# An FFT filter woven into a mixture layer: side products put behind other hosts, and their loads moved

## The chip, the cores and the metric

One core of one Trainium2 chip. TensorE (PE) multiplies, VectorE (DVE), ScalarE (ACT) and GpSimd (POOL) work on elements, SyncE (SP) issues nearly all transfers. The metric is the device time of one execution in microseconds, as a median of runs.

## What is computed

Eight batches of 3072 x 256 go through three stages:

```python
X = np.fft.rfft(x, axis=1)                        # stage 1: filter
y = np.fft.irfft(X * (filt_r + 1j * filt_i), n=x.shape[1], axis=1)
h = np.maximum(x @ w_in, 0.0)                     # stage 2: x is y, d_ff = 2048
x = h * h @ w_out
logits = x @ phi                                  # stage 3: 8 experts, 4 slots each
d = softmax(logits, over tokens); slot_input = d.T @ x
slot_out = per expert: np.maximum(slot_input @ w1, 0) @ w2
return softmax(logits, over slots) @ slot_out
```

## The kernel before

**Tiling.** 24576 tokens are 48 chunks of 512, six to a batch. A chunk takes eight pairs, a pair makes two blocks p0 and p1 of 128 hidden features: 12 full-array matmuls of 512 columns (L594 to L596, three products of split values). p0 and p1 each have one PSUM bank, so a block can start only when ACT's relu (L601) has read the one before. Square of p0 is on ACT (L603), square of p1 on POOL (L605), both transposed by DVE (L622). Eight squared blocks feed sixteen logit products (L663), whose result L leads to the softmax over tokens: evac_l (L712, L713), gather (L723, L724), emax (L729, L731), expo (L747), rescale (L753), turn_e, turn_l, slot_in (L794, the slots product), accum; then row_max, row_exp, row_out and store_c for the softmax over slots. The transposed hidden rows reach slot_in by 16 transfers a chunk (move, L651), each with an SP issue.

**The filter.** Its batch of 3072 points is factored into n1 = 128 by n2 = 24. mm_a (L165) is the forward product over n1, behind fold_x (L155 on DVE, L156 on POOL) and load_x, followed by evac_a (L172) and store_a (L181) to DRAM tensor S. load_s2 (L206) reads S turned; mm_b (L299) is the forward product over n2, then filt (L310), join (L319), mm_g2 (L218), evac_g2 (L228), store_g2 to DRAM tensor G. load_g (L460) reads G as gin for one group of 512 tokens, that is one chunk; mm_y (L514) is the inverse over n1, then even_y (L522), two unfolds (L531), and lead_y (L539, ACT) and rest_y (L546, POOL), which write the high and low half of xo, the next chunk's input, for k = 0 and 1. Groups 0, 1 and 6 take two transposing products (mm_ai, L478) instead.

**Order.** All engines run in the order in which the program issues instructions, written by hand. Time is counted in positions t: a pair is two, a half block 0.5, a chunk 16, a batch 96. Five streams of steps (dsp, mv, late, fft, w) each hold (t, step); at every half block run_streams fires what is due, steps without PSUM banks before the half block too, those with banks after it. Five side banks are shared. Positions below are counted within a chunk, so 9.5 is behind the second half of the fifth pair's p1. The logits come at 1.5 and 9.5; the slots product of the chunk before follows at 9.5, the gather at 3.5. Moves are due at 10 to 11.5, 14, 14.5, 2 and 2.5. In the steady state of batches 3 to 7, y comes at 9.5 behind the slots product; the b products (four a batch) once at 1.5 behind the logits and three times at 6 alone; the a products (three a batch) at 6 twice and at 1.5 once; g2 at 1.5. fft_events has the steps of one batch with three lists (TA: load, fold, product of each third; TB: b products; TG: g2) and lead times before them (LEAD: weights w, v, filter f, S). What a batch's filter does is laid over the chunks of the batch before.

Of the kernel before, what the change touches and what calls it, by code (L numbers as in the profile page):

```python
# [22 lines left out]
NCH = NB * NCB  # L23
# [15 lines left out]
def body(tc, x, cA, cAf, fwp, fwd, ivp, inv, flt, cst, w_in, w_out, phi, w1, w2, out):  # L39
# [83 lines left out]
    def fft_events(b, pl, put, TA, TB, TG, n, st):  # L123
# [263 lines left out]
        if b == 0:  # L387
# [21 lines left out]
            for i in range(8):  # L409
                put((.38, .4, .42, .44)[i] if i < 4 else F(i - 4) + 2.6, load_f, i)  # L410
                T = (16.8, 17.2, 20, 22.4, 24.9, 25.3, 27.4, 27.8)[i]
                for s in range(2):
                    put(T + .1 * s, mm_t, i, s)
                    put(T + .3 + .1 * s, evac_t, i, s)
                put(F(i) - 1.2, mm_b, i)
# [4 lines left out]
                put((29.85, 32.3, 34.75, 37.2, 39.9, 41.5, 44.6, 40.5)[i], mm_g, i)  # L420
                T = (31.1, 33.6, 36.1, 38.6, 41.2, 44.7, 45.9, 42.4)[i]
                for c in range(4):
                    put(T, evac_g, i, c)
                put(T + 1.25, store_g, i)
            return

        for s, (TL, TF, T) in enumerate(TA):
            put(TL, load_x, s)
            for k in range(2):
                put(TF + k, fold_x, s, k)  # L430
                for g in range(2):
                    put(T + 0.5 + (0 if T % 16 == 6 else 0.5) * k, evac_a, s, k, g)
                put(T + 2 + 0.5 * k, store_a, s, k)
            put(T, mm_a, s)
        LW, LV, LF, LS = n["lead"]
        for j in range(4):
            T = TB[j]
# [10 lines left out]
            T = TG[j]  # L448
# [5 lines left out]
    def out_events(b, st, late):  # L454

        def load_g(g):
            if b + g:
                t = G["mlp"].tile([128, 4, D], F32, tag="gin", name="gin", bufs=2)
                src, o = (st["G1"], 0) if (b, g) == (0, 1) else (st["G"], 4 * g - 8 * (b == 0))
                sync.dma_start(out=t, in_=src[:, o:o + 4, :])  # L460
            else:
                t = scratch("gi", 1, [128, 4, D])
                sync.dma_start(out=t[0:96], in_=st["Gu"])
                sync.dma_start(out=t[96:128], in_=st["Gz"])
            st["gi", g] = t

        def warm():

            p = side()
            for _ in range(6):  # L470
                pe.matmul(p[:, 0:416], cI, cst_t[:, 0:416], start=True, stop=True)
            done(p)

        def mm_ai(g, k):
            t = st["gi", g]
            p = side()
            for a in range(4):
                pe.matmul(  # L478
                    p[:, 128 * a:128 * a + 128], t[:, a, 128 * k:128 * k + 128], cI,
                    start=True, stop=True,  # L480
                )
            st["ai", g, k] = p

        def lead_ai(g, k):
            if k == 0:
                xo[b * NCB + g] = G["mlp"].tile([128, 2, 2, CH], F32R, tag="xo", name="xo", bufs=2)
            act.activation(
                out=xo[b * NCB + g][:, 0, k, :].rearrange("p (q a t) -> p a q t", q=4, a=4),
                in_=st["ai", g, k].rearrange("p (a q t) -> p a q t", a=4, q=4), func=ACTF.Copy,
            )  # L490

        def rest_ai(g, k):
            o = xo[b * NCB + g]
            p = st.pop(("ai", g, k))
            hi, lo = (
                a[:, n, k, :].rearrange("p (q a t) -> p a q t", q=4, a=4)
                for n, a in enumerate((o.bitcast(F32), o))
            )
            vec.tensor_tensor(
                out=lo, in0=p.rearrange("p (a q t) -> p a q t", a=4, q=4), in1=hi, op=ALU.subtract  # L500
            )
            done(p)

        def mm_y(g):
            t = st["gi", g]
            st["y", g] = p = [side() for e in range(2)]
            for a in range(4):
                for k in range(2):
                    for e in range(2):
                        for d in range(2):  # L510
                            rows = slice(64 * e, 64 * e + 64)
                            o = 128 * k + 64 * d
                            y = p[e][64 * d:64 * d + 64, D * k:D * k + D]
                            pe.matmul(  # L514
                                y.rearrange("p (q a t) -> p a q t", q=2, a=4)[:, a], t[rows, a, o:o + 64],
                                cI[rows, 0:64],
                                start=True, stop=True, skip_group_check=True, tile_position=(64 * e, 64 * d),
                            )

        def even_y(g):  # L520
            p = st["y", g][0]
            act.activation(  # L522
                out=st["gi", g][:, 2:4, :], in_=p.rearrange("p (k c) -> p k c", k=2), func=ACTF.Copy
            )
            done(p)

        def unfold(g, op):
            t = st["gi", g]
            p = st["y", g][1]
            o = t[:, 0:2, :] if op == ALU.add else t[:, 2:4, :]  # L530
            vec.tensor_tensor(out=o, in0=t[:, 2:4, :], in1=p.rearrange("p (k c) -> p k c", k=2), op=op)  # L531
            if op != ALU.add:
                done(p)

        def lead_y(g, k):
            if k == 0:
                xo[b * NCB + g] = G["mlp"].tile([128, 2, 2, CH], F32R, tag="xo", name="xo", bufs=2)
            o = xo[b * NCB + g][:, 0, k, :].rearrange("p (h c) -> p h c", h=2)
            act.activation(out=o, in_=st["gi", g][:, k::2, :], func=ACTF.Copy)  # L539

        def rest_y(g, k):
            o = xo[b * NCB + g]
            hi, lo = (
                a[:, n, k, :].rearrange("p (h c) -> p h c", h=2) for n, a in enumerate((o.bitcast(F32), o))
            )
            gps.tensor_tensor(out=lo, in0=st["gi", g][:, k::2, :], in1=hi, op=ALU.subtract)  # L546

        for g in range(NCB):
            if 6 * b + g not in (0, 1, 6):
                T = 96 * b + 16 * g - 6.5  # L550
                late(max(T - 19.5, 13.5), load_g, g)
                late(T, mm_y, g)
                late(T + 0.5, even_y, g)
                late(T + 1, unfold, g, ALU.add)
                late(T + 1, unfold, g, ALU.subtract)
                for k in range(2):
                    late(T + 2 + 2 * k, lead_y, g, k)
                    late(T + 2.5 + 2 * k, rest_y, g, k)
                continue
            T = 96 * b + 16 * g - 4  # L560
            put = late
            if T < 0:
                def put(t, fn, *a):
                    put0(ST["G0"] + ST["Gd"] * (t + 7), fn, *a)
            put(T - (5 if (b, g) == (0, 1) else 3), load_g, g)
            if T < 0:
                put(T - 1, warm)
            for k in range(2):
                put(T + k, mm_ai, g, k)
                put(T + k + 0.5, lead_ai, g, k)  # L570
                put(T + k + 0.5, rest_ai, g, k)
# [126 lines left out]
    def dispatch_events(c, put):  # L698
        q = 16 * (c + 1) + (2 if c else 6)
# [203 lines left out]
        else:  # L903
            put(q + 7.5, slot_in)
            put(q + 9, accum)
        put(q + 11, row_max)
        put(q + 13, row_exp)
        put(q + 14, row_out)
        put(q + 17, store_c)


    def f64(t, a, e):
# [192 lines left out]
    with tc.manual_schedule():  # L1105
        put, late = stream("fft"), stream("late")
# [24 lines left out]
        for n in range(4):  # L1131
# [2 lines left out]
                wput(WO[n][1][k], conv_wo, n, k)  # L1134

        LEAD = [
            [[6.5, 6.5, 9.5, 9.5], [10, 7.5, 8, 10], [5, 6, 6.5, 6.5], [5.5, 10.5, 10, 10]],
            [[5.5, 7.5, 15.25, 15.25], [6.5, 12.5, 13.5, 13.5], [5, 5.5, 10, 10], [5.5, 13, 15.25, 15.25]],
            [[20.25] + [15.25] * 3, [13.5] * 4, [20.5, 10, 10, 10], [6, 15.25, 15.25, 15.25]],
        ]  # L1140

        opened = False
# [6 lines left out]
        for b in range(1, NB):  # L1149
            st = {}  # L1150
            if b == 1:
                when = ([(22, 24.5, 26.5), (24, 29, 33.5), (27.5, 32, 36.5)], [47, 54.5, 65.5, 76.5], [53, 61.5, 70.5, 81.5])
            elif b == 2:
                when = ([(-19, -15.5, -10), (-11, -7, -3), (-5.5, -3, 0)], [13.5, 22, 38, 54], [18.5, 33.5, 49.5, 65.5])
            else:
                when = ([(-41, -31, -26), (-23, -19, -14.5), (-22.5, -15.5, -10)], [1.5, 22, 38, 54], [17.5, 33.5, 49.5, 65.5])
            fft_events(b, lambda: G["fft"], stream("fft", 96 * (b - 1)), *when, dict(f=3, u=8, c=2, lead=LEAD[min(b, 3) - 1]), st)
            out_events(b, st, late)
        for c in range(NCH - 1):
# [241 lines left out]
        for g in range(NG):  # L1401
            b, o = divmod(g, N2 // 4)
# [171 lines left out]
```

## Time and profile before

| | |
|---|---|
| median of 3 runs | 1855.48 us (1854.55 to 1858.27) |
| profiled execution | 1859.09 us, its span 1857.3 us |
| granted TensorE clock, mean | 0.996 |
| busy: PE, DVE, ACT, POOL | 98%, 65%, 56%, 42% of the span |
| chain that ended last | PE 84%, DMA 5%, DVE 3% |
| SP's DMA queue | 78.7% of 16 engines' span |

The span is what the profiler recorded of the profiled execution; its own time is 1.8 us longer. PE's busy share counts matmuls from start to modelled end, and these overlap; a pause between two starts shows as idle time in the timeline, with the releaser behind the arrow. A timeline row has start, duration, engine, line, operation, output and inputs, count.

### The profile page before, as it was taken

What the parts mean: (1) busy time and instruction counts of PE and PEld (TensorE: products, weight loads), DVE (VectorE), ACT (ScalarE), POOL (GpSimd) and SP (SyncE); (2) the same over time, 40 slices, a digit from 0 to 9 for tenths busy, and PEclk for the clock granted to TensorE, in tenths of its full rate; (3) what the DMA queues carried; (4) which work ended last, traced back from release to release, by engine and by line L of the source; (5) the groups of instructions that cost most, each with busy time, mean ns of one, the idle gap of its engine ahead of it and who ended that gap; (6) DMA issues with size and microseconds to landing.
All of it is one profiled execution on the core that took longest, in us unless ns stands there. A gap on an engine that the chain in (4) does not pass through costs nothing.

```text
span 1857.3 us, 42036 instructions
## 1 busy us (share of the span) xinstructions
PE 1812.1 (98%) x16326; PEld 1192.9 (64%) x16326; DVE 1212.9 (65%) x2267; ACT 1033.4 (56%) x1930; POOL 776.3 (42%) x812
## 2 busy tenths in 40 slices
PE   9899999999999999999999999999999999999987
PEld 6666666666666666666666666666566666666555
DVE  7856666676666666666667666666666756565558
ACT  6755555556555564555655555556555555555445
POOL 4043543454444534544444444354344443333224
PEclk9999999999999999999999999999999999999999
DMA  8669989878777896888778787687878666675999
GB/s 309 205 184 281 257 234 269 247 212 238 230 213 203 227 273 165 224 243 214 234 220 222 209 253 220 189 229 217 247 199 240 200 169 182 171 206 153 247 338 383
DMA packets 245813, 425.02 MB, mean 229 GB/s; under 512 B 25712, under 2 KB 103664, under 8 KB 245616
## 3 DMA queue, kind: packets, MB, share of 16 engines
q1 hardware_dynamic: 244744, 421.13, 78.7%
q8 instruction: 130, 2.13, 0.5%
q10 hardware_dynamic: 728, 1.15, 0.2%
q14 instruction: 67, 0.55, 0.1%
q0 software_dynamic: 144, 0.07, 0.0%
HBM read 151.71 MB, written 77.59 MB: 123 GB/s over the span
## 4 chain that ended last, share of the span: by engine, by line
PE 84%; DMA 5%; DVE 3%; SPq 2%; issue 2%; ACT 1%; POOL 1%; POOLq 0%; DVEq 0%; ACTq 0%
PE p L594 18%; PE p L595 17%; PE p L596 17%; PE L L663 9%; PE sd L794 8%; PE sd L218 3%; PE sd L299 3%; PE sd L514 2%; PE sd L165 2%; DMA f<-S 2%; SPq L651 1%; DMA hd<-hT 1%; DVE ct L1208 1%; PE pt L1197 1%; PE pt L1410 1%
## 5 line engine op out<-in xcount | busy, mean ns | idle before, releaser
L605 POOL TENSOR_TENSOR h<-h 128x512 f32<-128x512 f32 x375 | 395.1, 1054 | 837.0 <-ACT h L601 747.5
L601 ACT ACTIVATE h<-p 128x512 f32<-128x512 f32 x768 | 459.0, 598 | 348.9 <-PE p L596 334.5
L622 DVE STREAM_TRANSPOSE hT<-h 128x512 f32<-128x512 f32 x736 | 485.3, 692 | 250.4 <-ACT h L603 230.4
L594 PE MATMUL p<-xo,wiH 128*128 128x512 f32 x1534 | 621.7, 405 | 0.1
L595 PE MATMUL p<-xo,wiH 128*128 128x512 f32 x1534 | 605.6, 395 | 7.2 <-POOL xo L546 7.2
L596 PE MATMUL p<-xo,wiL 128*128 128x512 f32 x1534 | 605.8, 395 | 0.0
L594 PEld LDWEIGHTS p<-xo,wiH 128*128 128x128 f32 x1534 | 288.1, 188 | 122.4 <-issue 43.9
L595 PEld LDWEIGHTS p<-xo,wiH 128*128 128x128 f32 x1534 | 288.6, 188 | 70.0 <-POOL xo L546 9.4
L596 PEld LDWEIGHTS p<-xo,wiL 128*128 128x128 f32 x1534 | 288.3, 188 | 68.4
L603 ACT ACTIVATE h<-h 128x512 f32<-128x512 f32 x393 | 248.4, 632 | 12.5
L319 POOL TENSOR_TENSOR u<-u 128x256 f32<-128x256 f32 x224 | 160.5, 739 | 114.9 <-DVE u L310 114.9
L663 PE MATMUL L<-h,wf 128*32 128x512 f32 x1536 | 186.9, 599 | 2.2 <-DVE wf L1021 1.8
L531 DVE TENSOR_TENSOR gin<-gin,sd 128x512 f32<-128x512 f32 x90 | 61.8, 687 | 182.7 <-ACT gin L522 181.2
L522 ACT ACTIVATE gin<-sd 128x512 f32<-128x512 f32 x45 | 26.9, 598 | 256.7 <-PE sd L514 256.7
L794 PE MATMUL sd<-hd,eT 128*32 128x512 f32 x1472 | 166.3, 592 | 0.0
L310 DVE TENSOR_TENSOR u<-sd,f 128x512 f32<-128x512 f32 x240 | 152.7, 675 | 11.5 <-PE sd L299 10.1
L546 POOL TENSOR_TENSOR xo<-gin,xo 128x512 fp32r<-128x512 f32 x90 | 119.3, 1325 | 0.0
L794 PEld LDWEIGHTS sd<-hd,eT 128*32 128x32 f32 x1472 | 47.8, 110 | 110.1 <-issue 106.8
L228 ACT ACTIVATE f<-sd 128x512 f32<-128x512 f32 x112 | 61.1, 610 | 79.8 <-PE sd L218 79.8
L713 DVE TENSOR_TENSOR lo<-L,lp 128x512 fp32r<-128x512 f32 x47 | 32.3, 688 | 107.4 <-ACT lp L712 107.4
L663 PEld LDWEIGHTS L<-h,wf 128*32 128x32 f32 x1536 | 40.0, 109 | 96.2 <-issue 91.4
L770 DVE STREAM_TRANSPOSE eT<-et 32x128 f32<-32x128 f32 x184 | 72.0, 391 | 1.9
(161 smaller groups left out, 1596.2 us busy)
## 6 DMA issues: line engine op xcount, KB each, us to landing
hd<-hT SPq DMA_DIRECT2D x736, 256.0 KB
f<-flt SPq DMA_DIRECT2D x28, 1024.0 KB
gin<-G SPq DMA_DIRECT2D x47, 512.0 KB
out<-w1t SPq DMA_DIRECT2D x47, 512.0 KB
f<-x SPq DMA_DIRECT2D x84, 256.0 KB
S<-f SPq DMA_DIRECT2D x42, 512.0 KB
f<-S SPq DMA_DIRECT2D x112, 192.0 KB
G<-f SPq DMA_DIRECT2D x112, 192.0 KB
```

Source lines behind the costliest of these rows:

```text
L310: vec.tensor_tensor(out=u, in0=p.rearrange("p (h d) -> p h d", d=D), in1=f[:, 2 * r + k:2 * r + k + 1, :].to_broadcast([128, 2, D]), op=AL ...
L319: gps.tensor_tensor(out=a[:, h, :], in0=a[:, h, :], in1=b[:, 1 - h, :], op=ALU.add if h else ALU.subtract)
L546: gps.tensor_tensor(out=lo, in0=st["gi", g][:, k::2, :], in1=hi, op=ALU.subtract)
L594: pe.matmul(p, wh, x[:, 0, kk, :], start=(kk == 0), stop=False)
L595: pe.matmul(p, wh, x[:, 1, kk, :], start=False, stop=False)
L596: pe.matmul(p, wl, x[:, 0, kk, :], start=False, stop=(kk == 1))
L601: act.activation(out=h, in_=p, func=ACTF.Relu, scale=2.0 ** -8)
L603: act.activation(out=h, in_=h, func=ACTF.Square)
L605: gps.tensor_tensor(out=h, in0=h, in1=h, op=ALU.mult)
L622: vec.transpose(hT[c, f // 8][:, f // 4 % 2, :, o:o + 128], h2[P, k].rearrange("p (b t) -> p b t", b=4))
L663: pe.matmul(lg[c][32 * n:32 * n + 32, :], wf[:, f, :], h2.pop((P + n // 2, n % 2)), start=(f < 4), stop=(f >= FT - 4), tile_position=(0, 3 ...
L794: pe.matmul(S[32 * n:32 * n + 32, :], e[:, 32 * t:32 * t + 32], v, start=(t == 0), stop=(t == 3), tile_position=(0, 32 * n),)
```

## The change

The b products of every batch from the second on come at 9.5, behind the slots product; two of the three a products too, the other at 1.5 behind the logits. y comes at 3.5 directly behind the gather, but for groups 2, 3 and 6. Group 6 (first of the second batch) goes by mm_y like the others. The loads of S, weights, filter, x and G come due between 3 and 6, the folds at 6, 7 and 12, 13. An a product at 9.5 has its copies to SBUF (evac_a) two by two at 11.5 and 13.5 and its stores at 13 and 15. row_max, row_exp and row_out come 2.5 later, store_c 1 later, but for the last two chunks.

```diff
--- before.py
+++ after.py
@@ -428,9 +428,10 @@
             put(TL, load_x, s)
             for k in range(2):
                 put(TF + k, fold_x, s, k)
+                slow = T % 16 == 9.5
                 for g in range(2):
-                    put(T + 0.5 + (0 if T % 16 == 6 else 0.5) * k, evac_a, s, k, g)
-                put(T + 2 + 0.5 * k, store_a, s, k)
+                    put(T + (2 + 2 * k if slow else 0.5 + 0.5 * k), evac_a, s, k, g)
+                put(T + (3.5 + 2 * k if slow else 2 + 0.5 * k), store_a, s, k)
             put(T, mm_a, s)
         LW, LV, LF, LS = n["lead"]
         for j in range(4):
@@ -546,9 +547,9 @@
             gps.tensor_tensor(out=lo, in0=st["gi", g][:, k::2, :], in1=hi, op=ALU.subtract)
 
         for g in range(NCB):
-            if 6 * b + g not in (0, 1, 6):
-                T = 96 * b + 16 * g - 6.5
-                late(max(T - 19.5, 13.5), load_g, g)
+            if 6 * b + g > 1:
+                T = 96 * b + 16 * g - {2: 9, 3: 6.5, 6: 6.5}.get(6 * b + g, 12.5)
+                late(max(96 * b + 16 * g - {6: 10, 7: 24}.get(6 * b + g, 26), 13.5), load_g, g)
                 late(T, mm_y, g)
                 late(T + 0.5, even_y, g)
                 late(T + 1, unfold, g, ALU.add)
@@ -562,7 +563,7 @@
             if T < 0:
                 def put(t, fn, *a):
                     put0(ST["G0"] + ST["Gd"] * (t + 7), fn, *a)
-            put(T - (5 if (b, g) == (0, 1) else 3), load_g, g)
+            put(T - (5 if g else 3), load_g, g)
             if T < 0:
                 put(T - 1, warm)
             for k in range(2):
@@ -903,10 +904,11 @@
         else:
             put(q + 7.5, slot_in)
             put(q + 9, accum)
-        put(q + 11, row_max)
-        put(q + 13, row_exp)
-        put(q + 14, row_out)
-        put(q + 17, store_c)
+        d = 2.5 if c < NCH - 2 else 0
+        put(q + 11 + d, row_max)
+        put(q + 13 + d, row_exp)
+        put(q + 14 + d, row_out)
+        put(q + 17 + (d > 0), store_c)
 
 
     def f64(t, a, e):
@@ -1134,9 +1136,9 @@
                 wput(WO[n][1][k], conv_wo, n, k)
 
         LEAD = [
-            [[6.5, 6.5, 9.5, 9.5], [10, 7.5, 8, 10], [5, 6, 6.5, 6.5], [5.5, 10.5, 10, 10]],
-            [[5.5, 7.5, 15.25, 15.25], [6.5, 12.5, 13.5, 13.5], [5, 5.5, 10, 10], [5.5, 13, 15.25, 15.25]],
-            [[20.25] + [15.25] * 3, [13.5] * 4, [20.5, 10, 10, 10], [6, 15.25, 15.25, 15.25]],
+            [[6.5, 6.5, 9.5, 9.5], [10, 7.5, 8, 7.5], [5, 6, 6.5, 6.5], [5.5, 10.5, 10, 10]],
+            [[6] * 4, [13.5] * 4, [14, 5.5, 5.5, 5.5], [4, 6.5, 6.5, 6.5]],
+            [[6] * 4, [13.5] * 4, [21, 5.5, 5.5, 5.5], [6.5] * 4],
         ]
 
         opened = False
@@ -1149,11 +1151,11 @@
         for b in range(1, NB):
             st = {}
             if b == 1:
-                when = ([(22, 24.5, 26.5), (24, 29, 33.5), (27.5, 32, 36.5)], [47, 54.5, 65.5, 76.5], [53, 61.5, 70.5, 81.5])
+                when = ([(22, 24.5, 26.5), (24, 29, 33.5), (27.5, 32, 36.5)], [47, 54.5, 65.5, 76.5], [53, 61.5, 73.5, 81.5])
             elif b == 2:
-                when = ([(-19, -15.5, -10), (-11, -7, -3), (-5.5, -3, 0)], [13.5, 22, 38, 54], [18.5, 33.5, 49.5, 65.5])
+                when = ([(-19, -15.5, -12.5), (-13, -10, -6.5), (-8, -4, 1.5)], [9.5, 25.5, 41.5, 57.5], [17.5, 33.5, 49.5, 65.5])
             else:
-                when = ([(-41, -31, -26), (-23, -19, -14.5), (-22.5, -15.5, -10)], [1.5, 22, 38, 54], [17.5, 33.5, 49.5, 65.5])
+                when = ([(-29, -26, -22.5), (-28, -20, -14.5), (-13, -10, -6.5)], [9.5, 25.5, 41.5, 57.5], [17.5, 33.5, 49.5, 65.5])
             fft_events(b, lambda: G["fft"], stream("fft", 96 * (b - 1)), *when, dict(f=3, u=8, c=2, lead=LEAD[min(b, 3) - 1]), st)
             out_events(b, st, late)
         for c in range(NCH - 1):
```

## Rows read from the trace of the kernel before

**Rows 1.** which lines PE waited for, whole span; us in total, times, longest us.

```profile
PE p L595 <- POOL xo L546: 7.2, 5, 1.4
...
PE sd L299 <- DMA f<-S: 4.1, 9, 1.0
...
PE sd L478 <- DMA gin<-G: 0.8, 1, 0.8
```

**Rows 2.** timeline of PE, start and duration in us, at one xo stall.

```profile
1318.91 0.40 PE L594 MATMUL p<-xo,wiH 128*128 128x512 f32 x1
1320.75 0.50 PE L595 MATMUL p<-xo,wiH 128*128 128x512 f32 x1 [1.44 <-POOL xo L546]
```

**Rows 3.** timeline of PE around a later L299 bundle of that batch.

```profile
1439.15 0.40 PE L596 MATMUL p<-xo,wiL 128*128 128x512 f32 x1
...
1439.48 1.96 PE L299 MATMUL sd<-f,fw 48*32 48x256 f32 x64
1441.36 0.50 PE L594 MATMUL p<-xo,wiH 128*128 128x512 f32 x1
...
1441.70 0.39 PE L595 MATMUL p<-xo,wiH 128*128 128x512 f32 x1
```

**Rows 4.** timeline of POOL at the same xo stall.

```profile
1313.75 1.04 POOL L605 TENSOR_TENSOR h<-h 128x512 f32<-128x512 f32 x1 [8.60 <-ACT h L601]
1314.75 1.35 POOL L546 TENSOR_TENSOR xo<-gin,xo 128x512 fp32r<-128x512 f32 x1
1316.73 1.30 POOL L156 TENSOR_TENSOR f<-f 128x512 f32<-128x512 f32 x1 [0.63 <-DMA hd<-hT]
1317.99 1.49 POOL L605 TENSOR_TENSOR h<-h 128x512 f32<-128x512 f32 x1
1319.44 1.26 POOL L546 TENSOR_TENSOR xo<-gin,xo 128x512 fp32r<-128x512 f32 x1
```

**Rows 5.** timeline of PE at the first L299 bundle of the last batch.

```profile
1360.08 0.59 PE L299 MATMUL sd<-f,fw 48*32 48x256 f32 x2
...
1363.73 0.50 PE L594 MATMUL p<-xo,wiH 128*128 128x512 f32 x1
```

**Rows 6.** timeline of SP's queue, time of issuing, ahead of that bundle.

```profile
1336.76 0.32 SPq L181 DMA_DIRECT2D S<-f  x1
1345.85 8.15 SPq L651 DMA_DIRECT2D hd<-hT  x8
1354.05 3.38 SPq L206 DMA_DIRECT2D f<-S  x4
```

**Rows 7.** timeline of ACT, one chunk.

```profile
1295.78 0.60 ACT L601 ACTIVATE h<-p 128x512 f32<-128x512 f32 x1
1296.28 0.68 ACT L747 ACTIVATE et<-sd,nm 128x512 f32<-128x512 f32 x1
1296.84 0.20 ACT L747 ACTIVATION_READ_ACCUMULATOR et<-sd,nm 128x1 f32 x1
...
1300.69 0.28 ACT L753 ACTIVATE sc<-nm 128x1 f32<-128x1 f32 x1
...
1311.41 0.60 ACT L601 ACTIVATE h<-p 128x512 f32<-128x512 f32 x1 [0.93 <-PE p L596]
1312.04 0.63 ACT L603 ACTIVATE h<-h 128x512 f32<-128x512 f32 x1
1312.58 0.61 ACT L539 ACTIVATE xo<-gin 128x512 fp32r<-128x512 f32 x1
```

**Rows 8.** timeline of PE in that chunk.

```profile
1303.34 1.92 PE L663 MATMUL L<-h,wf 128*32 128x512 f32 x16
...
1309.71 0.50 PE L594 MATMUL p<-xo,wiH 128*128 128x512 f32 x1
```

**Rows 9.** timeline of DVE at the xo stall.

```profile
1314.86 1.79 DVE L155 TENSOR_TENSOR u<-f 128x512 f32<-128x512 f32 x1
```

## The prediction

> **What bounds the kernel now.** I read the page's busy times first: TensorE (PE) is busy nearly the whole span, so a change of order can gain no more than the holes in PE's stream and the price of its switches. The list of PE's waits then says where the holes are [rows 1]. Those outside the main loop (weights, tail) the change doesn't touch. Of those it touches, two are large. PE waits 7.2 us in five places for the low half of xo from GpSimd (POOL), and at least 4.1 us in nine pieces for rows of S read back from DRAM (`f<-S`). A third, 0.8 us, stands before the two transposing products of group 6.
>
> The first is read in two timelines. PE's matmul L595 starts 1.84 us after its forerunner [rows 2] where neighbours are 0.23 apart; the start behind a pause comes 0.34 later instead of 0.23, as it does behind a bundle [rows 3], so a place costs 1.6 + 0.1 = 1.7 us. POOL shows why: rest_y k=0 (L546), a fold (L156), a square (L605) slowed to 1.49, and only then rest_y k=1, whose end, 1319.44 + 1.26 = 1320.70, comes 0.05 before PE's start at 1320.75 [rows 2, 4]. Ahead of that fold POOL had idled 0.63.
>
> The second shows in the length of L299's first bundle in five batches (3 to 7); that of the last batch takes 1363.73 - 1360.08 = 3.65 us [rows 5], against 1441.36 - 1439.48 = 1.88 where the data are there [rows 3]. SP's queue has the reason: after a store at 1336.76 it issues nothing until 1345.85, then eight moves of hidden rows (8.15 us), and only behind them the four loads of S, from 1354.05 to 1357.4 [rows 6]; PE wants them at 1360.
>
> **The sum** is made as a difference to the profiled execution (1859.09 us; its span is 1857.3, so 1.8 lies around it). That run is 3.6 us above the median of the runs, 1855.48; I put the same difference on the median. About 0.2%, 3.7 us, is what a measurement of this kernel can tell from no change.
>
> **1. The xo stall goes.** The folds of batches 3 to 7 move from the chunk's edge to positions 6, 7 and 12, 13, and y to 3.5, so rest_y runs at 6 and 8, some seven units before the next chunk reads xo. 5 x 1.7 = **-8.6 us**. What is late next: step 6.
>
> **2. The S stall goes.** The loads of S come due at 3 and those of weights, filter, x and gin at 3 to 6, behind the last moves (2.5) and ahead of the next (10). SP has a hole of 1345.85 - 1337.08 = 8.8 us there [rows 6]; the four S loads need 3.38 of it. Some eight others at the same 0.85 would fill the hole and push the moves by a microsecond or two. I cost that at nothing: the last moves are due 7.5 positions, some 10 us, before the slots product reads their rows. If that cover fails, the wait comes back. Five times the excess of the bundle shown, 5 x 1.77: **-8.9 us**.
>
> **3. Group 6** no longer takes two transposing products alone, but one y product, loaded three units earlier: 0.8 of waiting [rows 1] and one bundle's edges, **-1.0 us**.
>
> **4. Edges.** A bundle between main matmuls costs an entry and an exit: L596 to L299 0.33 instead of 0.23, and L594 to L595 behind it 0.34 [rows 3], 0.2 us together. Before, y rode behind slot_in, and 35 bundles stood alone (three b and two a products in each of seven batches). After, 44 y products stand alone behind the gather, and one a product; all b products ride behind slot_in. I count the gather, a full-array product, as main matmul. Net ten more: **+2.0 us** (-2.4, if y needs no entry edge there, to +4, if the gather's exit costs one as well).
>
> **5. ScalarE (ACT) in positions 4 to 9, in 44 chunks.** The y work used to come after the exponential; now it comes on top of it. The steps are read from ACT's timeline [rows 7]; zero is the first main matmul behind y, at 1309.71 there [rows 8]. Relu p0 starts 1.70 later (1311.41), the square +0.63, lead_y k=0 +0.54, relu p1 +0.50, exp +0.50 (as from 1295.78 to 1296.28), the next relu +0.76 (exp and its accumulator read, to 1297.04), square +0.63, rescale +0.54, lead_y k=1 +0.18 (its 0.28 less the usual overlap of 0.1), relu p1 +0.50: it starts at 6.48 and ends at 7.08. PE wants that bank, with the handover of 0.05 seen above, after 30 matmuls: 30 x 0.233 + 0.11 = 7.10, against 7.13. So the relu is late by 0.03 and PE pays the restart of 0.1 as well. The two unfolds on VectorE (DVE), behind emax, end close to when lead_y wants them, which can only add. Bounds: 0 (a slip of 0.03 is within what the steps are good for) to 0.35; I take 0.15, near the sum, 44 x 0.15 = **+6.6 us** (0 to 15). Behind the waiting matmul stands all of PE.
>
> **6. POOL ahead of the logits at 9.5, in the 11 chunks with folds at 6 and 7** (one for batch 2, two each for 3 to 7). The new queue on POOL is square, rest_y k=0, two folds, square of the last pair, rest_y k=1; the logits need that last square. With the durations of the POOL timeline [rows 4]: relu p1 ends near 4.0, square to 5.0, rest_y to 6.35, two folds of 1.26 from where DVE's half of the fold permits, square 1.04. DVE's half (L155) took 1.79 us beside an L546, starting 0.11 behind it and ending after it [rows 4, 9]. Held to 6.35 likewise it ends near 7.0; the folds end at 9.55, the square at 10.6. PE wants it after 36 matmuls, the entry edge and half of the bundle of sixteen logits [rows 8], 36 x 0.233 + 0.2 + 0.9 = 9.5: 1.1 late, of which step 5 has 0.15. If DVE's half is done early, the folds start at 6.35 and the wait is 0.4. From 0.4 to 1.4; I take 1.0, since the held case is the one the row shows: 11 x 1.0 = **+11.0 us** (4 to 15).
>
> The Trainium skill, page "SBUF — State Buffer", section "SBUF: two separate sides", says that a DVE instruction with two SBUF inputs and a GpSimd instruction exclude each other for a whole instruction. By that rule L155 waits out the L546, and the trace agrees, since there it took 1.79 us [rows 9]; by it this step would be 11 x 1.1, without it 11 x 0.4.
>
> **7. Slow evacuations.** The a product at 9.5 in the same 11 chunks has its four L172 copies in two pairs, each ahead of a relu p1. By the steps of [rows 7]: relu p0 1.70 behind the product, square at 2.33, copies at 2.87 and 3.37, relu p1 from 3.87 to 4.45, handover 4.50. PE wants the bank after 18 matmuls, 18 x 0.233 + 0.11 = 4.30: 0.2 late, and the restart, 11 x 0.3 = **+3.3 us** (0 to 5).
>
> **8. Transition of batches 1 and 2**, and the later row_max, row_exp, row_out and store_c: each of the latter lies beside idle DVE and ACT. In the transition the steps of two schedules meet at odd positions, as where the 0.8 of [rows 1] stands now; two or three such waits are **+2.0 us** (0 to 4). Head and tail are unchanged.
>
> **Sum:** -8.6 - 8.9 - 1.0 + 2.0 + 6.6 + 11.0 + 3.3 + 2.0 = +6.4 us: **1861.9 us**.
>
> **Rivals.**
> *A, the margins hold; not slower.* One mechanism: the queue of squares and relus keeps the lead that PE's bundles give it, so ACT's 0.03 vanishes and POOL's folds start at once. It decides where the relu of step 5 ends before 7.05. Steps 5 and 7 are then 0, step 6 is 11 x 0.4 = 4.4: -18.5 + 2.0 + 4.4 + 2.0 = -10.1, 1845.4 us. For it: the margin is a few hundredths. Against it: step 6 doesn't hang on it.
> *B, DVE sets ACT's pace.* Emax, nm and two unfolds stand between the gather and lead_y; if they run 0.2 late, every chunk pays 0.35: 44 x 0.2 = +8.8 on the forecast, 1870.7 us. For it: y and emax fall into the same two microseconds. Against: emax is released by the gather on PE, so DVE's chain starts with PE and not later.
> *C, the loads still queue.* If moves keep SP when the S loads come due, the 8.9 us are not had: 1870.8 us. For it: they are still on one queue with the moves. Against: the hole of rows 6.
>
> **How the numbers follow.** Forecast 0.52, A 0.26, B 0.14, C 0.08. The forecast's own range, from its terms' bounds taken half at a time, is 1855 to 1869, of which a fifth lies within 0.2% and very little below. A spreads from 1840 to 1855 with a fifth of it within 0.2%. That gives faster by over 0.2% 0.24, within 0.2% 0.22, slower 0.54. To leave no more than two in ten out, the range takes in the nearer half of A and B's centre: 1845 to 1872.
>
> **What would show it.** Step 1: no PE wait for xo L546. Step 2: no wait for `f<-S`, all L299 bundles 1.9 us. Step 5: short waits of L594 for ACT's L601, three pairs behind each y. Step 6: L663 waiting about 1 us for POOL's L605, 11 times. Step 7: L594 waiting behind L172. The forecast is wrong if the waits for L601 and L605 add up to less than 10 us, or if the S wait is still there.

## The result, and the profile after

The changed kernel takes 1875.2 us as a median of 5 runs (1874.5 to 1880.1), against 1855.48: 1.010 times the time before, with a 95% interval of 1.0085 to 1.0116. It was forecast 6.4 us slower, with a range that ended at 1872; it is 19.7 us slower. The side was right and the size was not.

The profiled execution took 1880.07 us (span 1878.2) and is itself 4.9 us above its median; some of that lies in the tail, where one wait of 2.7 us that the profile puts down to nothing (`PE pt L837 <- issue`) stands, and the kernel before has none. To keep such differences out I compare stretches of the main loop, from the start of the main matmul at one position to that at another, read off PE's timeline of each profiled execution:

| stretch, positions | before | after | difference |
|---|---|---|---|
| 48 to 112, transition from batch 1 to 2 | 151.53 | 162.02 | +10.5 |
| 112 to 656, 34 chunks of the steady schedule | 1209.56 | 1216.07 | +6.5 |
| 656 to 736, no filter left but y | 157.24 | 158.24 | +1.0 |
| all | 1518.33 | 1536.33 | +18.0 |

The list of PE's waits after the change (us in total, times, longest; lines of the changed kernel stand one or two higher: L594 is now L595, L605 is L606, L663 is L664, L713 is L714, L724 is L725, while L299, L218, L155 and L156 keep their numbers):

```profile
PE L L664 <- POOL h L606: 6.7, 9, 2.3
...
PE sd L725 <- DVE lo L714: 2.5, 2, 1.8
...
PE L L664 <- DMA gin<-G: 0.8, 1, 0.8
...
PE p L595 <- ACT h L602: 0.6, 1, 0.6
...
PE p L596 <- POOL xo L547: 0.5, 1, 0.5
```

Of the three holes of [rows 1] two are gone: no wait for `f<-S` is listed, and none for `gin<-G` ahead of the products of group 6. Of the five waits for xo one of 0.5 us is left. In their place stand the logits waiting for POOL's square, nine times, and a tenth time in the same place of a chunk, listed under `gin<-G`; all ten lie between positions 112 and 656. In the transition the gather waits for lo (the low half of L, written by DVE), a wait that the list of the kernel before doesn't have. There is one listed wait for ACT's relu, of 0.6 us and in the transition too, where the forecast had 44 short ones. Waits as short as those can be missing from this list, as e5_yonly shows below, so the lengths of the chunks have to tell.

The waits for lo have a sequel in this execution. Behind two of them, in which PE stood 1.6 us (and 0.5 more ahead of y) and 1.8 us, the granted TensorE clock fell to the lower of its two levels, 1.2 GHz instead of 2.4: it was 0.50 from 221.7 to 225 us and from 262.6 to 266. Main matmuls start 0.43 us apart there instead of 0.23, first eight of them and then four:

```profile
221.93 0.63 PE L596 MATMUL p<-xo,wiH 128*128 128x512 f32 x1
222.36 0.63 PE L597 MATMUL p<-xo,wiL 128*128 128x512 f32 x1
```

That is 1.6 and 0.9 us, and the a product ahead of the four takes 0.8 longer, so about 3.3 us of the transition's 10.5 are the clock. The kernel before, e7_oldtrans, e8_best and e9_spread have no such fall between positions 48 and 736; e1, e2, e3 and e4 have one each, in the transition and directly behind a wait of PE of 2.0 to 2.4 us. Not every wait has one behind it: that of 2.3 us for the square, at 1141 us, hasn't. The mean granted clock of the changed kernel's other four executions is 0.995 or 0.996 where this one has 0.993, so they may have fewer falls.

### The profile page after: what moved, and what is told of

It is laid out like the page before. It is cut to its first block, busy times and chain, and to the rows that moved or that the text cites. A ratio compares the mean times of both kernels' runs of the same rounds, so it can differ in the third digit from the quotient of the medians.

```text
span 1878.2 us, 42092 instructions
## 1 busy us (share of the span) xinstructions
PE 1831.6 (98%) x16374; PEld 1206.2 (64%) x16374; DVE 1213.3 (65%) x2267; ACT 1028.6 (55%) x1931; POOL 775.9 (41%) x814
## 4 chain that ended last, share of the span: by engine, by line
PE 80%; issue 4%; DMA 4%; DVE 4%; SPq 3%; POOL 3%; ACT 2%; POOLq 0%; DVEq 0%; ACTq 0%
PE p L595 17%; PE p L597 16%; PE p L596 16%; PE sd L795 9%; PE L L664 8%; PE sd L299 3%; DMA f<-x 2%; PE sd L218 2%; PE sd L515 2%; SPq L652 2%; POOL f L156 1%; PE sd L165 1%; SPq L143 1%; POOL h L606 1%; DMA hd<-hT 1%
## 5 line engine op out<-in xcount | busy, mean ns | idle before, releaser
L606 POOL TENSOR_TENSOR h<-h 128x512 f32<-128x512 f32 x375 | 390.9, 1045 | 797.8 <-ACT h L602 675.3
L595 PE MATMUL p<-xo,wiH 128*128 128x512 f32 x1534 | 626.6, 408 | 0.7 <-ACT h L602 0.6
L595 PEld LDWEIGHTS p<-xo,wiH 128*128 128x128 f32 x1534 | 288.8, 188 | 141.9 <-issue 51.5
L664 PE MATMUL L<-h,wf 128*32 128x512 f32 x1536 | 197.8, 599 | 9.8 <-POOL h L606 6.7
L795 PE MATMUL sd<-hd,eT 128*32 128x512 f32 x1472 | 173.9, 592 | 0.0
L795 PEld LDWEIGHTS sd<-hd,eT 128*32 128x32 f32 x1472 | 61.6, 110 | 97.8 <-issue 82.6
L547 POOL TENSOR_TENSOR xo<-gin,xo 128x512 fp32r<-128x512 f32 x92 | 118.9, 1293 | 0.3 <-ACT xo L540 0.3
L664 PEld LDWEIGHTS L<-h,wf 128*32 128x32 f32 x1536 | 41.3, 109 | 113.1 <-issue 91.2
L714 DVE TENSOR_TENSOR lo<-L,lp 128x512 fp32r<-128x512 f32 x47 | 32.4, 690 | 88.1 <-ACT lp L713 88.1
L856 DVE SCALAR_TENSOR_TENSOR ac<-ac,sc,sd 128x512 f32<-128x512 f32 x46 | 34.1, 742 | 69.6 <-PE sd L795 69.6
L761 DVE STREAM_TRANSPOSE lt<-sd 32x128 f32<-32x128 f32 x192 | 60.0, 312 | 24.7 <-ACT et L748 22.6
```

The costliest lines, as they stand in the source:

```text
L595: pe.matmul(p, wh, x[:, 0, kk, :], start=(kk == 0), stop=False)
L606: gps.tensor_tensor(out=h, in0=h, in1=h, op=ALU.mult)
L664: pe.matmul(lg[c][32 * n:32 * n + 32, :], wf[:, f, :], h2.pop((P + n // 2, n % 2)), start=(f < 4), stop=(f >= FT - 4), tile_position=(0, 3 ...
L795: pe.matmul(S[32 * n:32 * n + 32, :], e[:, 32 * t:32 * t + 32], v, start=(t == 0), stop=(t == 3), tile_position=(0, 32 * n),)
```

## Experiments

Each run below changed due times of the changed kernel, or in one case of the kernel before. Times are medians of several runs where an interval stands; stretches are those of the table above, each from one profiled execution. The kernel before, run again beside e1, e2, e3 and e7, took 1857.2 us instead of 1855.48, so a difference of two medians from different groups is uncertain by some 2 us.

**e2_folds: the folds behind the square.**

```diff
-                when = ([(-29, -26, -22.5), (-28, -20, -14.5), (-13, -10, -6.5)], ...
+                when = ([(-29, -24.25, -22.5), (-28, -20, -14.5), (-13, -8.25, -6.5)], ...
```

(and likewise -10 to -8.25 for batch 2)

> The changed kernel with the folds of positions 6 and 7 put 1.75 later, behind the square of the fourth pair on GpSimd, in all 11 chunks that have them. Theory: the logits at 9.5 wait (with the slots product behind them stretched: 1.6 us in the fifth, 2.0 us in the sixth chunk of a batch) because this square is queued behind the folds; then these waits go and nothing takes their place, since the a product that needs the folds comes 5 us after the logits start: -17 to -20 us, 1855 to 1858 us. Rival: the folds are late because x lands late, and the a product or rest_y behind them becomes the wait: less than -8 us.

Measured: 1856.8 us, 1.000 of the kernel before (0.999 to 1.0013), 18 us less than with the change as it was. From 112 to 656 it takes 1196.55 us, 19.5 less than the changed kernel and 13.0 less than the kernel before. The fifth and sixth chunk of a batch go from 37.35 and 37.98 us on average to 35.74 and 35.70. Nothing took the place of the wait. The POOL timeline of the two kernels in the sixth chunk of the last batch says it in rows (start, duration, idle before and releaser); first the changed kernel:

```profile
1348.75 1.04 POOL L606 TENSOR_TENSOR h<-h 128x512 f32<-128x512 f32 x1 [3.77 <-ACT h L602]
1349.75 1.29 POOL L547 TENSOR_TENSOR xo<-gin,xo 128x512 fp32r<-128x512 f32 x1
1351.83 1.29 POOL L156 TENSOR_TENSOR f<-f 128x512 f32<-128x512 f32 x1 [0.79 <-DMA S<-f]
1353.74 1.28 POOL L156 TENSOR_TENSOR f<-f 128x512 f32<-128x512 f32 x1 [0.62 <-DVE u L155]
1354.99 1.04 POOL L606 TENSOR_TENSOR h<-h 128x512 f32<-128x512 f32 x1
```

then with the folds later:

```profile
1329.37 1.04 POOL L606 TENSOR_TENSOR h<-h 128x512 f32<-128x512 f32 x1 [3.78 <-ACT h L602]
1330.36 1.29 POOL L547 TENSOR_TENSOR xo<-gin,xo 128x512 fp32r<-128x512 f32 x1
1332.37 1.04 POOL L606 TENSOR_TENSOR h<-h 128x512 f32<-128x512 f32 x1 [0.72 <-ACT h L602]
1333.37 1.29 POOL L547 TENSOR_TENSOR xo<-gin,xo 128x512 fp32r<-128x512 f32 x1
1335.29 2.90 POOL L156 TENSOR_TENSOR f<-f 128x512 f32<-128x512 f32 x2 [0.63 <-DVE u L155]
```

The second square ends 7.3 us behind the start of the first in the one, 4.0 in the other, where POOL even idles 0.72 us for the relu. On PE in the changed kernel (same chunk) the logits start at 1353.33 and have to stop for it:

```profile
1353.33 1.92 PE L664 MATMUL L<-h,wf 128*32 128x512 f32 x14
1356.08 0.62 PE L664 MATMUL L<-h,wf 128*32 128x512 f32 x1 [0.83 <-POOL h L606]
1356.40 0.59 PE L795 MATMUL sd<-hd,eT 128*32 128x512 f32 x1
...
1356.63 4.07 PE L795 MATMUL sd<-hd,eT 128*32 128x512 f32 x31
1360.63 0.65 PE L165 MATMUL sd<-u,ca_t 64*64 64x512 f32 x2
```

From 1353.33 to 1360.63 are 7.30 us; in chunks without folds the same two products take 1.74 + 3.55 = 5.29. So this place costs 2.0 us, though only 0.83 of it is listed as idle before one matmul: that idle time is counted from the end of the fourteen logits ahead, and the slots product behind takes 4.23 us from its first start to the a product instead of 3.55.

**e3_xearly: x landed before the folds.**

```diff
-                when = ([(-29, -26, -22.5), (-28, -20, -14.5), (-13, -10, -6.5)], ...
+                when = ([(-31, -26, -22.5), (-28, -20, -14.5), (-15, -10, -6.5)], ...
```

> The changed kernel with the loads of x that the folds of positions 6 and 7 wait for issued two positions earlier in batches 3 to 7, ahead of the last four moves, folds where they are. Theory A: the folds wait for x to land (VectorE idles 0.4 and 0.6 us for it), so with x there the folds run back to back and the ten waits of 1.6 and 2.0 us fall to about 0.8: -9 to -12 us, 1863 to 1866 us. Theory B, that of the prediction: the durations on GpSimd and the port alone make the wait, so the time moves by less than 3 us. Both: the moves come some 3.7 us later; if that uncovers them, the slots product waits for their rows.

Measured: 1873.0 us (1.0063 to 1.0106 of the kernel before), 2.2 less than the changed kernel, and 3.3 less from 112 to 656. Theory A falls; the median keeps B's bound of 3 us and the stretch just misses it. In the sixth chunk of a batch the loads no longer count (37.25 to 37.45 us, like the fifth), and 1.6 us of wait is left in both (37.35 less 35.45 and the 0.3 of the copies). In the changed kernel the late x cost the sixth chunk 0.1 to 0.4 us in four batches and 2.0 in one, where DVE idled 1.91 us for `f<-x` at 1136.12. What is left is in two timelines, POOL and DVE of the sixth chunk of the last batch, zero (the first main matmul behind y) at 1342.24:

```profile
1347.28 1.29 POOL L547 TENSOR_TENSOR xo<-gin,xo 128x512 fp32r<-128x512 f32 x1
1349.20 1.68 POOL L156 TENSOR_TENSOR f<-f 128x512 f32<-128x512 f32 x1 [0.63 <-DVE u L155]
...
1352.08 1.04 POOL L606 TENSOR_TENSOR h<-h 128x512 f32<-128x512 f32 x1
```

```profile
1346.90 1.29 DVE L761 STREAM_TRANSPOSE lt<-sd 32x128 f32<-32x128 f32 x4 [0.36 <-ACT et L748]
1348.22 0.89 DVE L155 TENSOR_TENSOR u<-f 128x512 f32<-128x512 f32 x1
1348.22 1.49 DVE L155 TENSOR_TENSOR u<-f 128x512 f32<-128x512 f32 x2
```

DVE's half begins only behind its own four transposes of L (L761), at 1348.22, and is held a little by POOL's L547 (0.89 us instead of 0.69; the last row holds DVE's halves of both folds). POOL's first fold then starts beside DVE's second half and takes 1.68 us instead of 1.28. The square ends at 1353.12, 10.9 us behind zero.

**e7_oldtrans: the transition as before.**

```diff
-                T = 96 * b + 16 * g - {2: 9, 3: 6.5, 6: 6.5}.get(6 * b + g, 12.5)
+                T = 96 * b + 16 * g - (6.5 if 6 * b + g < 11 else 12.5)
...
-        d = 2.5 if c < NCH - 2 else 0
+        d = 2.5 if 9 < c < NCH - 2 else 0
...
```

(with the lists of batches 1 and 2, their lead times and group 6 as in the kernel before)

> The changed kernel from the third batch on, but with the due times of the kernel before for the first two batches' filter, groups 1 to 10, and the row steps of chunks 0 to 9. Theory: the transition alone costs 10.5 us of the loss (from 167 to 329 us), so it goes to 1864 to 1866 us, and the five batches keep their excess of 1.5 us each. Rival: the transition's waits come from the third batch's steps, which overlap it and stay: less than -4 us.

Measured: 1866.2 us, 1.0043 of the kernel before (1.0028 to 1.0057), 9.0 less than the changed kernel and just above the range of the theory. The transition takes 153.7 us instead of 162.0; the stretch behind it stays, at 1213.6 against 1216.1. So nearly half of the whole loss of the change, 8.3 of 18.0 us, came from the due times in four chunks, the two falls of the clock among it.

**e1_rows: the row steps at their old due times.**

```diff
-        d = 2.5 if c < NCH - 2 else 0
+        d = 0
```

> The changed kernel with row_max, row_exp, row_out and store_c back at their old due times, nothing else. Theory: in the transition (the three chunks before and the one behind 290 us) the gather waits because row_out, 1.6 to 2 us of work, now stands on VectorE ahead of lo; then the gather's waits at 175, 219 and 261 us (0.8, 1.8 and 2.0 us) fall by some 4 to 6 us in all and the time to 1869 to 1871 us. Rival: the transposes and folds that wait for transfers there are late by themselves and row_out only fills their pause; then the time falls by less than 1.5 us. In the chunks of batches 3 to 7 both expect no change, since VectorE idles over 2 us ahead of lo there.

Measured: 1874.4 us (1.0071 to 1.0124 of the kernel before), only 0.8 less; but the median over four runs is uncertain by more than that, and by it the rival would hold; the profile tells more. The transition goes from 162.0 to 157.8 us. Its first two chunks go from 40.89 and 41.81 us to 38.74 and 38.41, -5.6 us, as the theory has it, though 1.6 of that is the clock, which doesn't fall in these chunks in e1_rows; the third goes from 43.16 to 44.48. The cause of the gain is in DVE's timeline of the changed kernel, in the second chunk:

```profile
214.32 1.31 DVE L623 STREAM_TRANSPOSE hT<-h 128x512 f32<-128x512 f32 x2 [3.94 <-DMA hd<-hT]
215.55 1.25 DVE L310 TENSOR_TENSOR u<-sd,f 128x512 f32<-128x512 f32 x2
216.72 0.27 DVE L873 TENSOR_REDUCE sm<-ce 128x4 f32<-128x128 f32 x1
...
217.89 0.56 DVE L876 TENSOR_TENSOR co<-ce,sm 128x128 f32<-128x128 f32 x1
218.37 0.68 DVE L714 TENSOR_TENSOR lo<-L,lp 128x512 fp32r<-128x512 f32 x1
```

The transposes wait 3.94 us for the moves to free their buffer, and row_out (L873 to L876) now stands behind that pause and ahead of lo: 1.65 us on the way to the gather. In the kernel before it ran ahead of the pause:

```profile
209.26 0.24 DVE L872 TENSOR_REDUCE sm<-ce 128x4 f32<-128x128 f32 x1
...
212.55 1.30 DVE L622 STREAM_TRANSPOSE hT<-h 128x512 f32<-128x512 f32 x2 [2.18 <-DMA hd<-hT]
...
214.96 0.67 DVE L713 TENSOR_TENSOR lo<-L,lp 128x512 fp32r<-128x512 f32 x1
```

After the change the gather's second product, which should follow in 0.23, starts two microseconds behind the first (PE, same place):

```profile
217.08 0.40 PE L724 MATMUL sd<-lp,ss_t 128*128 128x512 f32 x1
219.10 0.50 PE L725 MATMUL sd<-lo,ss_t 128*128 128x512 f32 x1 [1.62 <-DMA iv<-inv]
```

(The releaser named there, a load of iv, isn't it: lo ends at 219.05, 0.05 ahead.) In the third chunk the gain comes back, because PE now reaches the logits sooner and the folds of batch 2 still wait for x (DVE idles 1.80 and 1.49 us for `f<-x` ahead of 264.78 and 266.96); in e1_rows PE reads

```profile
270.05 0.62 PE L664 MATMUL L<-h,wf 128*32 128x512 f32 x1 [2.26 <-POOL h L606]
```

and behind that wait the clock falls (0.50 from 271.4 to 274.8 us).

**e4_both: both of these.** Edits of e2_folds and e1_rows together.

> The changed kernel with both the folds of positions 6 and 7 put 1.75 later and the row steps back at their old due times, the transition's products where the change put them. Theory: the transition's loss of 10.5 us is row_out ahead of lo (4 to 6 us) and folds that wait for x ahead of a square (3 to 5 us), so the stretch from 48 to 112 positions takes 153 to 155 us instead of 162.0. Rival: it is the loads' new order on SyncE's queue, and the stretch stays above 157 us.

Measured, in one execution: 1853.2 us, 1512.1 from 48 to 736, so 6 us below the kernel before on the same stretch. The transition takes 157.1 us, at the rival's bound: the third chunk is still at 43.4 us. There the square is no longer late, but the y product of group 6 comes sooner than its load:

```profile
273.14 0.47 PE L515 MATMUL sd<-cst_t,gin 64*64 64x64 f32 x17 [2.43 <-DMA gin<-G]
```

SP issues the gin loads of groups 6 and 7 at 268.6 and 269.5 in that run. Ahead of the first it stands idle from 265.7, since the loads wait for the four stores of G to land (`SPq L461 <- DMA G<-f: 2.7, 2, 2.2` between 264 and 270 us); whether these stores were late by the order on SP's queue, as the rival has it, wasn't tested. Behind PE's wait the clock falls in this run too (0.50 from 273.9 to 277.2 us; five main matmuls lose 1.1 us). So the transition's loss has three layers, row_out ahead of lo, folds ahead of the square, and group 6's load behind the stores of G; each was hidden by the one above it.

**e5_yonly: y alone moved.** The kernel before, with y at 3.5 from group 7 on.

```diff
-                T = 96 * b + 16 * g - 6.5
-                late(max(T - 19.5, 13.5), load_g, g)
+                T = 96 * b + 16 * g - (12.5 if 6 * b + g > 6 else 6.5)
+                late(max(96 * b + 16 * g - 26, 13.5), load_g, g)
```

> The kernel before with y alone moved to 3.5, behind the gather, from group 7 on, all else in its old place. The prediction's step on ScalarE: each of 41 chunks pays 0.15 us for a late relu besides the two edges of a lone product of 0.2 us, together +14 us, less the xo stall of 8.6. What the changed kernel's chunks without other stalls show (35.45 us, and ScalarE ahead of the relu by 0.08 us): no late relu, +8.2 us for the edges, -8.6 us for the xo stall, so within 2 us of the kernel before from 112 to 656 positions and +0.2 us in each of the last five chunks.

Measured, in one execution: 1872.2 us, and 1220.7 from 112 to 656, 11.2 above the kernel before. In chunks without another stall ScalarE's part came as the profile had it and not as the prediction had it: they go from 35.43 to 35.62 or 35.66, the last five from 31.45 to 31.65, so 0.2 us for the edges of a lone product and nothing for a relu. But the fifth and sixth chunk of a batch do have the late relu. There the four copies of the a product at 6 (L172, 2.07 us) stand in ACT's queue as well, PE's weight load (PEld) waits for the relu, PE starts 0.18 us late and the start behind it comes 0.1 later, as behind any pause; the fifth chunk goes from 35.44 to 35.89. In the last batch:

```profile
1308.03 2.07 ACT L172 ACTIVATE f<-sd 128x512 f32<-128x512 f32 x4 [0.25 <-PE sd L165]
```

```profile
1312.49 0.19 PEld L594 LDWEIGHTS p<-xo,wiH 128*128 128x128 f32 x1 [0.45 <-ACT h L601]
```

The list of PE's waits has no line for it. The first chunk of a batch shows some 0.2 us of the same. The xo stall goes as well (37.10 to 35.83, the late relu included). What the expectation missed besides is the wait for S, which the move alone makes worse:

```profile
PE sd L299 <- DMA f<-S: 5.9, 12, 1.5
```

against 4.1 in nine pieces in [rows 1]. The five chunks with that bundle take 35.9 to 39.5 us in place of 34.6 to 35.6; 0.2 of it is the edges, some 2 us the wait with what follows it; in the two longest of the five the granted clock falls as well (0.50 from 507.4 to 510.8 us and from 1152.6 to 1159.3). SP's queue shows why the wait grows. The moves ahead of these loads are released by the end of the slots product (SP's longest wait there is for L794) and are issued 0.06 us behind it in both kernels. With y behind the slots product that end lies 9.52 us ahead of the chunk that wants S, without y 8.40. So the loads, behind the moves, come later against PE:

```profile
1363.84 3.10 SPq L206 DMA_DIRECT2D f<-S  x4
```

This is 0.17 behind the start of the chunk at 1363.67, where in the kernel before the first load, at 1354.05 [rows 6], was 1.26 ahead of the start at 1355.31. So y in its old place had given the loads 1.1 of these 1.4 us. Moved alone, it loses more at b than it gains at xo.

**e8_best and e9_spread: the repairs together.** e8_best has e7_oldtrans's transition and e2_folds's folds from batch 3 on. e9_spread adds:

```diff
-                    put(T + (2 + 2 * k if slow else 0.5 + 0.5 * k), evac_a, s, k, g)
+                    put(T + (2 + 2 * k + 0.5 * g if slow else 0.5 + 0.5 * k), evac_a, s, k, g)
```

> The two repairs together: the due times of the kernel before in the transition (as in e7_oldtrans) and, from the third batch on, the changed schedule with the folds of positions 6 and 7 put 1.75 later (as in e2_folds). If the two causes are separate, their gains add up: the stretch from 48 to 736 positions takes 153.7 + 1196.6 + 158.2 = 1508 us against 1518.3 in the kernel before, and the time is 1846 to 1849 us, faster than both kernels. Rival: with the folds mended the third batch's steps collide with the old transition, and it gives back more than 4 us.

> As e8_best, with the four copies behind an a product at 9.5 spread over four half pairs (11.5, 12, 13.5, 14) instead of two by two. Theory: the two copies ahead of a relu make it 0.2 us late, and PE pays 0.27 to 0.31 us twice per batch and once more each for two pairs, so 35.72 us chunks go to 35.45: -2.5 to -3 us against e8_best. Rival: the first copy alone makes the relu late enough, or the later banks hold up something else: within 0.5 us.

Measured: 1848.7 us, 0.994 of the kernel before (0.992 to 0.996), for e8_best, and 1845.7 us, 0.992 (0.990 to 0.994), for e9_spread, the two on one chip with a median of 1858.9 for the kernel before. From 48 to 736 e8_best takes 1507.6 us, within 1 us of the sum expected. Both beat both kernels. The spread copies bring the fifth and sixth chunk from 35.74 and 35.70 to 35.43, -2.9 us from 112 to 656 (1196.84 to 1193.94). Of that, 2.3 us comes back in the transition of that profiled execution, where the schedules of the two kernels are the same; the medians differ by 3.0. ACT's timeline shows how. In the changed kernel two copies stand together ahead of a relu:

```profile
1365.37 1.07 ACT L172 ACTIVATE f<-sd 128x512 f32<-128x512 f32 x2
1366.32 1.28 ACT L602 ACTIVATE h<-p 128x512 f32<-128x512 f32 x2
```

with e9_spread one stands ahead of it and one behind:

```profile
1338.84 0.58 ACT L172 ACTIVATE f<-sd 128x512 f32<-128x512 f32 x1
1339.32 0.59 ACT L602 ACTIVATE h<-p 128x512 f32<-128x512 f32 x1
1339.80 0.60 ACT L172 ACTIVATE f<-sd 128x512 f32<-128x512 f32 x1
```

## Why the prediction was right and wrong

**Steps 1 and 2, the two stalls: right, in cause and size.** From 112 to 656 they held 5 x 1.67 and 5 x 1.74 us of the time before (37.10 against 35.43, and 35.09 on average against 33.35 for a chunk with no lone product but a filter), 17.1 us in all where 17.5 were forecast, and both are gone.

**Step 4, edges: right.** In the changed kernel's rows the entry behind a full-array gather (0.32 instead of 0.23) and the exit (0.34) cost 0.1 each, and the last five chunks, where y is all that differs, are each 0.2 longer:

```profile
1343.30 0.39 PE L725 MATMUL sd<-lo,ss_t 128*128 128x512 f32 x1
1343.62 1.16 PE L515 MATMUL sd<-cst_t,gin 64*64 64x64 f32 x64
1344.71 0.50 PE L595 MATMUL p<-xo,wiH 128*128 128x512 f32 x1
1345.05 0.39 PE L596 MATMUL p<-xo,wiH 128*128 128x512 f32 x1
```

In PE's timelines from chunk 1 to 46 there are 42 lone bundles before and 53 after, so the net count of ten was near, though not its parts: it left out lone g2 products, and the b products of the second batch, which the section on the change has at 9.5, kept their places.

**Step 5, ACT: wrong, 6.6 us too much.** The relu that should end at 7.08 behind zero, 0.03 late, ends at 6.97, 0.08 ahead of the 7.05 at which it would be in time. ACT in the changed kernel, zero at 1344.71:

```profile
1348.09 0.58 ACT L602 ACTIVATE h<-p 128x512 f32<-128x512 f32 x1
1348.57 0.68 ACT L748 ACTIVATE et<-sd,nm 128x512 f32<-128x512 f32 x1
1349.14 0.20 ACT L748 ACTIVATION_READ_ACCUMULATOR et<-sd,nm 128x1 f32 x1
1349.23 0.59 ACT L602 ACTIVATE h<-p 128x512 f32<-128x512 f32 x1
...
1351.10 0.58 ACT L602 ACTIVATE h<-p 128x512 f32<-128x512 f32 x1
```

The step that failed is "the next relu +0.76": I added the read of the accumulator in full, while the next relu starts 0.09 behind its start, 0.66 behind the exponential's. Rows of operations that wait for others ([rows 7] has the next operation idle) give no spacing for a full queue. With 0.66 the sum has all 44 relus 0.07 early. The chunk lengths agree: a chunk without waits is 35.45 us against 35.43, with one lone bundle in either, so some 0.02 us is left of the 0.15. e5_yonly shows how thin the margin is: with the copies of an a product in ACT's queue the wait that I had forecast is there, in the fifth and sixth chunks. The changed kernel has no copies there: they come at 2 and 2.5, or at 11.5 and later. I had named 0.03 as within the error and still priced it at 0.15 in every chunk.

**Step 6, POOL: the mechanism right, the size short.** The square queued behind the folds is what held the logits; e2_folds takes the waits away by order alone. But a place cost 1.6 and 2.2 us in the mean of the fifth and sixth chunks (their periods of 37.35 and 37.98 less 35.45 and the 0.3 of step 7), so 19 us in ten places against 10 forecast; 1.5 of it is the one late landing of x at 1136 us. What the working lacked, from the e3_xearly rows: its square ended at 10.6 and there ends at 10.9, mostly because POOL's first fold starts beside DVE's second half and is held 0.4 by it; I had the hold on one side only. With the 0.1 taken off for step 5 and 0.1 for the restart, which I left out here and counted elsewhere, that makes 1.5 of the fifth chunk's 1.6. That DVE's half ends near 7.0 was right by luck: I had it held by L546, and it ends at 6.9 because it starts only at 6.0, behind four transposes, and is held by 0.2. In the sixth chunk the rest is x that lands late (two waits of DVE for `f<-x`, 0.40 and 0.58 us in the last batch); I had put the loads' timing at no cost, with the slots product as the one to suffer. The rule of the Trainium skill, page "SBUF — State Buffer", section "SBUF: two separate sides", that the two instructions exclude each other whichever starts first, agrees with the trace here in both directions: L155 at 1348.22 took 0.89 behind an L547, L156 at 1349.20 took 1.68 behind an L155. They end 0.54 and 1.17 us behind the end of the one that held them, 0.1 to 0.15 less than the 0.69 and 1.28 that they take alone.

**Step 7, copies: right.** ACT's rows above give a relu that starts 3.81 behind zero (1362.51) where the working had 3.87, and the place costs 0.3; e9_spread gives it back.

**Steps 3 and 8, the transition: wrong, 8 us too little.** I put it at +1.0 together, with 1.3 more for its share of steps 6 and 7, and called row_max, row_exp, row_out and store_c free because they lie beside idle DVE. That is so in the steady chunks, where DVE waits for lp ahead of lo. In the transition DVE's pause lies earlier, ahead of transposes that wait for moves, and what is put behind that pause is on the way to the gather. I had not followed those rows in the trace of the kernel before, where the same transposes wait 2.2 us with row_out ahead of them. Nor had the working a term for the clock, about 3.3 us in the profiled execution, which fell behind these waits. +10.5 was measured; e7_oldtrans gives 8.3 of it back.

The sum put right: +6.4, less 6.6 for step 5, plus 9 for step 6 in ten places, plus 8 for the transition, is +17; the stretch measured +18.0, and the last 1 us is open. By its own sign the forecast is wrong too: the listed waits for the relu and the square are 0.6 and 6.7 us, under 10. But the sign read listed idle time, and the ten places of the square cost 19. Rival A's condition for ACT came true and its condition for POOL didn't; rivals B and C are out, by the early relu and by the missing wait for S. The range was too short because the bounds that mattered, 15 for step 6 and 4 for step 8, were drawn from one event each.

## What to carry to other kernels

When a step is put later on an engine that works in order, ask for each engine not whether it idles but where: work moved from before a pause to behind it lands on the path, and the same move is free in the steady state and costs microseconds in the chunks where two schedules overlap. Work that nobody waits for until much later goes behind the operation that the bottleneck needs next; here 1.75 positions for a fold were worth 18 us. Ask too what a step gives time to where it stands: y behind the slots product gave the loads of S 1.1 us. And cost the start-up and transition stretches by their own rows, not as a few times the steady state.

## What the runs showed of the hardware

The exponential with its sum takes two ACT instructions of 0.68 and 0.20 us, but a relu behind it starts 0.66 us after its start, so the read is nearly hidden when the queue is full. DVE and POOL held each other in either direction: DVE's fold took 1.79 us [rows 9] and 0.89 in place of 0.69 where POOL had begun first, POOL's 1.68 in place of 1.28 where DVE had. A wait for one square shows as 0.83 us of idle time where the two products together run 2.0 us over, so the length of the whole bundle has to be read, not its idle time. And behind waits of PE of 1.6 to 2.4 us the granted clock was 0.50, the lower of its two levels, and main matmuls started 0.43 us apart instead of 0.23; behind another of 2.3 us it stayed at 1.
